# One instruction per step on both blocks of a unit's h, in a pair of PSUM banks, and the reciprocal held in SBUF

## The chip, the cores and the metric

The kernel runs on one core of one Trainium2 chip. The metric is the time of one execution in microseconds (us) on the device: the median of three runs of the kernel before is 825.93 us (825.08 to 829.08). Five engines work side by side, each through its own queue in order: TensorE (PE in the profile, with PEld for its loads of stationary data), VectorE (DVE), ScalarE (ACT), GpSimd (POOL) and SyncE (SP), which issues all of this kernel's DMAs. They meet only at semaphores. Data lie in SBUF, and results of TensorE in PSUM, which has eight banks of 512 fp32 values in each of 128 partitions.

## The reference

Two attentions and a layer with a rational function in place of an activation, all in fp32:

```python
def sm_attn(qq, kk, vv):
    s = scale * np.matmul(qq, kk.transpose(0, 1, 3, 2))
    a = np.exp(s - np.max(s, axis=-1, keepdims=True))
    return np.matmul(a / (np.sum(a, axis=-1, keepdims=True) + 1e-09), vv)
p_packed = sm_attn(p, k, v)               # 32 packed queries per head
x = sm_attn(q, p_packed, p_packed)        # 8 batches, 8 heads of 64, 576 rows each -> 4608 x 512
h = x @ w_in                              # 512 -> 2048
P = a[0] + a[1] * h + a[2] * h**2 + a[3] * h**3
Q = 1.0 + np.abs(b[0]) * np.abs(h) + np.abs(b[1]) * h**2
out = (P / (Q + 1e-6)) @ w_out            # 2048 -> 512
```

The weights come as 64-bit words and are taken apart into fp32 on the chip.

## The kernel before

**Units.** The work behind the attention is cut into 128 units: 8 batches, two halves of 288 rows each (HALF), and 8 chunks of 256 of the 2048 columns of h. `hidden` (line 644) builds one unit as a generator with yields in between. A unit has two blocks, f = 0 and 1, of 128 columns of h. For each block TensorE adds six matmuls (w_in and x are each split into a high and a low part, and three of the four products are taken) into one bank `h` of 128 x 288 values; there are two such banks (h_ring, line 299). From each block, one after the other, lines 659 to 664:

- ScalarE writes Y = a3*h + a2 and U = |b0*h|, and, after the first ten units, the square b1*h*h into a buffer `sq`;
- VectorE makes Y = Y*h and then Y = (Y + a1)*h.

So each of these instructions works on 288 columns and is issued twice in a unit. Behind both blocks, GpSimd adds U and sq (line 670), and from here all work on 576 columns at once: ScalarE writes V = ln(U + 1) and V = exp(-V) (lines 674, 675), a first reciprocal of Q, and VectorE takes three steps: Y = (Y + a0)*V, V = (U + 1)*V, and Y = (2 - V)*Y (lines 676, 677, 679), the numerator times the reciprocal with a step of refinement. **V lies in PSUM**, in the one pair of banks of V_ring (line 300). At last `split` (line 371) rounds Y to a high part gh on ScalarE and takes gl = Y - gh on GpSimd, and GpSimd copies the last 32 of the 288 rows' values to G, to be multiplied later (`remainder`). In the first ten units ("early": while the weights are still converted) no square is taken; there VectorE makes U = (U + b0)*h for each block (line 668) and ScalarE its absolute value, so GpSimd adds nothing.

`acc_block` (line 719) multiplies gh and gl by the parts of w_out, three units later (LAG), into two banks `acc`.

**Around it.** `attention` (line 456) of the next batch, and `m_chunk`, which multiplies the packed values by w_in, are put between the units and use the two banks `at`. `convert` (line 375) takes the words of the weights apart in the first 150 us: on VectorE with a shift-and-or (`w<-w`, `m<-m`) and an integer addition (`w<-w,w`, `win<-w,win`, `win<-m,win`) on 128 x 1024 words, each with two operands in SBUF.

**The order.** All operations go to a planner (lines 32 to 202), not straight to the engines. It knows a cost for each (line 40) and the dependences (line 100; in PSUM any two accesses of one buffer by different engines are ordered, in the order in which the code states them, reads too: line 120), plays a list schedule forward and backward four times, and issues in the order of the best. An instruction on one engine costs it the same whatever the other engines are doing. Buffers go round in rings (line 218): two for U, three for Y, one for sq and one pair of banks for V.

The eight banks are: two acc, two h, two V, two at.

Of the kernel before, what the change touches and what calls it, by code (L numbers as in the profile page):

```python
# [14 lines left out]
F32R = mybir.dt.float32r  # L15
# [3 lines left out]
AF = mybir.ActivationFunctionType  # L19
ALU = mybir.AluOpType  # L20
# [3 lines left out]
P = 128  # L24
# [209 lines left out]
def attention_rational_ffn(  # L234
# [32 lines left out]
    sb = ctx.enter_context(tc.tile_pool(name="sb", bufs=1))  # L267
    ps = ctx.enter_context(tc.tile_pool(name="ps", bufs=1, space=PSUM))
    tc.nc.scalar.preload_act_table_set("natural_log_exp_and_others")
    nc = Planner(tc.nc)  # L270


    ident = sb.tile([P, P], F32, name="ident")
    make_identity(tc.nc, ident)
    neg = sb.tile([P, P], F32R, name="neg")
    ab, abS, one, root = (sb.tile([P, n], F32, name=x) for n, x in ((6, "ab"), (7, "abS"), (1, "one"), (5, "root")))
    win = sb.tile([P, NCH, NCC, CF], F32, name="win")
    G = sb.tile([P, NFC, 2 * REM], F32, name="G")
# [4 lines left out]
    o_ring = Ring(sb, "o", 1, [P, 2, DM])  # L283

    full_ring = Ring(sb, "full", 1, [P, DM])
    nat_ring = Ring(sb, "nat", 2, [P, 4 * NS * D])
    pn_ring = Ring(sb, "pn", 1, [P, NG, D])
    rkq_ring = Ring(sb, "rkq", 1, [P, H, D])
    rv_ring = Ring(sb, "rv", 1, [REM, H, D])

    kx_ring = Ring(sb, "kx", 1, [P, NJ, T])
    ppT_ring = Ring(sb, "ppT", 2, [P, P])
    AH_ring, AL_ring = (Ring(sb, x, 2, [P, NG, T], F32R) for x in ("AH", "AL"))

    m_ring = Ring(sb, "m", NCH // 2, [P, 2, NG, 2 * CF], F32R)
    U_ring, U2_ring, Y_ring = (Ring(sb, x, n, [P, 2, HALF]) for x, n in (("U", 2), ("sq", 1), ("Y", 3)))
    gh_ring, gl_ring = (Ring(sb, x, 2, [P, 2, HMAIN], F32R) for x in ("gh", "gl"))
    acc_ring = Ring(ps, "acc", 2, [P, DM])
    h_ring = Ring(ps, "h", 2, [P, 512])
    V_ring = Ring(ps, "V", 1, [P, 2, 512])  # L300
    at_ring = Ring(ps, "at", 2, [P, 512])


# [107 lines left out]
    def load(bb, what):  # L411
        if bb >= B:
            return
        if what == "rem":

            r, rv, pn = NAT[bb, "r"], NAT[bb, "rv"], NAT[bb, "p"] = rkq_ring.next(), rv_ring.next(), pn_ring.next()
            nc.sync.dma_start(r[0:REM], k[bb, :, NS * P : T, :].rearrange("h p d -> p h d"))
            for j in range(NJ):
                nc.sync.dma_start(pn[32 * j : 32 * j + 32], p[bb, NG * j : NG * j + NG].rearrange("r n d -> n r d"))
            nc.sync.dma_start(r[REM : 2 * REM], q[bb, :, NS * P : T, :].rearrange("h p d -> p h d"))  # L420
            nc.sync.dma_start(rv, v[bb, :, NS * P : T, :].rearrange("h p d -> p h d"))
            return
# [32 lines left out]

    def attention(bb):
        pT, eTr, m2, st = (small[:, x:y] for x, y in zip(cuts, cuts[1:]))
        eTr = eTr[0:REM]
        m2 = m2.rearrange("p (a b) -> p a b", a=3)

        mx, nb, sm, f, fs, F = (st[:, 4 * i : 4 * i + 4] for i in range(6))
# [61 lines left out]
        for r in range(NG):  # L523
            t = bank(bb)
            for s in range(NS):
                nc.tensor.transpose(t[:, s * P : (s + 1) * P], KX[:, r, s * P : (s + 1) * P], ident)
            nc.scalar.copy(KX[:, 2 + r, 0 : NS * P], t)
            if r == 1:
                t = bank(bb)
                for i in range(NG):  # L530
                    nc.tensor.transpose(t[0:REM, i * P : (i + 1) * P], KX[:, i, NS * P : T], ident)
                nc.scalar.copy(eTr, t[0:REM, 0 : NG * P])
            yield

        t = bank(bb)
# [1 line left out]
        for r in range(NG):  # L537
            for x, blocks in enumerate((range(2), range(2, NS + 1))):
                o = slice((2 * r + x) * D, (2 * r + x + 1) * D)
                tiles(  # L540
                    (
                        (
                            t[32 * j : 32 * j + 32, o],
                            KX[:, 2 + r, s * P + 32 * j : s * P + 32 * j + 32] if s < NS else eTr[:, r * P + 32 * j : r * P + 32 * j + 32],
                            NAT[bb, f"v{j // 2}"][:, 2 * (j % 2) + r, s, :] if s < NS else rv[:, 2 * j + r, :],
                        ),
                        dict(start=s == blocks[0], stop=s == blocks[-1]),
                    )
                    for s in blocks
                    for j in range(NJ)  # L550
                )
# [92 lines left out]
    def hidden(bb, x, c):  # L644
        ah, al = AH[bb], AL[bb]
        mh, ml = (M[bb, c // 2][:, i, :, c % 2 * CF : (c % 2 + 1) * CF] for i in range(2))
        early = converted < len(words)
        U, V, Y = U_ring.next(), V_ring.next()[:, :, 0:HALF], Y_ring.next()
        U2 = None if early else U2_ring.next()
        for f in range(2):  # L650
            h = h_ring.next()[:, 0:HALF]
            for i, (w, a) in enumerate(((mh, ah), (ml, ah), (mh, al))):
                for g in range(NG):
                    nc.tensor.matmul(
                        h, w[:, g, f * P : (f + 1) * P], a[:, g, x * HALF : (x + 1) * HALF],
                        start=g == 0 and i == 0, stop=g == NG - 1 and i == 2,
                    )
            u, y = U[:, f, :], Y[:, f, :]
            nc.scalar.activation(y, h, AF.Identity, scale=reg_a3, bias=a2)
            nc.scalar.activation(u, h, AF.Abs, scale=reg_b1 if early else reg_b0)  # L660
            if not early:
                nc.scalar.activation(U2[:, f, :], h, AF.Square, scale=reg_root)
            nc.vector.tensor_mul(y, y, h)
            nc.vector.scalar_tensor_tensor(y, y, a1, h, ALU.add, ALU.mult)


            if early:
                nc.vector.scalar_tensor_tensor(u, u, b0, h, ALU.add, ALU.mult)
            elif f == 1:
                nc.gpsimd.tensor_add(U, U, U2)  # L670
            yield
        if early:
            nc.scalar.activation(U, U, AF.Abs)
        nc.scalar.activation(V, U, AF.Ln, bias=one)
        nc.scalar.activation(V, V, AF.Exp, scale=-1.0)
        nc.vector.scalar_tensor_tensor(Y, Y, a0, V, ALU.add, ALU.mult)
        nc.vector.scalar_tensor_tensor(V, U, (1.0 + 1e-6) * S, V, ALU.add, ALU.mult)
        yield
        nc.vector.scalar_tensor_tensor(Y, V, 2.0, Y, ALU.subtract, ALU.mult, reverse0=True)
        gh, gl = GS[bb, x, c] = gh_ring.next(), gl_ring.next()  # L680
        split(Y[:, :, 0:HMAIN], gh, gl)
# [91 lines left out]
    def stage(u):  # L773
        if u in pipe:
            next(pipe[u])

    def filler(i):
        if i in mt:
            m_chunk(*mt[i])
        for x in fill.get(i, ()):  # L780
            next(x)

    for u in range(NU + LAG + 2):
        if u < NU:
            pipe[u] = hidden(*units[u])
        stage(u)
        if 0 <= u - LAG < NU:
            acc_block(u - LAG, 0)
        filler(2 * u)
        stage(u)  # L790
        stage(u - 2)
# [39 lines left out]
```

## Time and profile before

| | |
|---|---|
| median of the runs, us | 825.93 |
| lowest and highest of the runs, us | 825.08, 829.08 |
| the profiled execution's own time, us | 828.38 |
| its span (first to last instruction), us | 826.6 |
| granted TensorE clock, mean | 0.965 |
| PE, PEld busy, us | 768.0, 605.5 |
| DVE, ACT, POOL busy, us | 694.3, 690.4, 459.5 |

A row of the profile that groups instructions names line, engine, operation, out<-in by the program's names, shapes out<-in, and the count; then the busy time of the group in us, the mean of one instruction in ns, and the idle time of the engine just before them with what ended it. All instructions have the line 202, since the planner issues them there; they are told apart by names. `Y<-Y,abS,V` is the step with a0 (abS holds the coefficients), `V<-U,V` and `Y<-V,Y` the two behind it, `Y<-Y,h` and `Y<-Y,abS,h` the two on h.

### The profile page before, as it was taken

To read this page: it belongs to the slowest core of one execution; us is meant where nothing else is said; L and a number is where in the kernel's file an instruction comes from. 1 tells how busy PE (TensorE), PEld (TensorE's weight loads), DVE (VectorE), ACT (ScalarE), POOL (GpSimd) and SP (SyncE) were. 2 spreads that over 40 slices of the span, in tenths; PEclk is the share of its full clock that TensorE was granted. 3 is DMA by queue.
4 is the path that set the end of the run, shared out by engine and by line. 5 is a ranking of instruction groups with operands and counts; after the bars stand their busy time and mean duration, and the time that the engine had idled before them with its cause. 6 is when DMAs were issued, how large, how long until landed. Compare 5 with 4: busy or idle time off the path is not lost.

```text
span 826.6 us, 15104 instructions
## 1 busy us (share of the span) xinstructions
PE 768.0 (93%) x5424; PEld 605.5 (73%) x5424; DVE 694.3 (84%) x1296; ACT 690.4 (84%) x1558; POOL 459.5 (56%) x454
## 2 busy tenths in 40 slices
PE   5467688899999999999999999999999999999997
PEld 3244365687877788788878788788877878778885
DVE  1899998888898688988898788988898778998873
ACT  3799787799988889899888888999888878898872
POOL 0003644675568445665577455765568446856663
PEclk9797698899999999999999999999999999999999
DMA  8994344001410116010510206010600211000001
GB/s 179 329 307 124 114 98 90 26 26 56 95 54 0 56 39 122 27 52 30 110 38 1 78 17 122 26 55 27 123 27 1 77 40 28 26 1 26 26 1 38
DMA packets 99834, 56.01 MB, mean 68 GB/s; under 512 B 82736, under 2 KB 90928, under 8 KB 99760
## 3 DMA queue, kind: packets, MB, share of 16 engines
q1 hardware_dynamic: 99760, 55.06, 25.2%
q8 instruction: 42, 0.69, 0.4%
q14 instruction: 32, 0.26, 0.1%
HBM read 45.62 MB, written 9.44 MB: 67 GB/s over the span
## 4 chain that ended last, share of the span: by engine, by line
PE 75%; DVE 12%; ACT 9%; issue 2%; DMA 1%; POOL 1%; SPq 0%; DVEq 0%; ACTq 0%; POOLq 0%
PE acc L202 37%; PE h L202 22%; PE at L202 16%; DVE Y L202 4%; DVE w L202 3%; DVE small L202 2%; ACT Y L202 1%; ACT U L202 1%; ACT V L202 1%; ACT m L202 1%; ACT w L202 1%; ACT kx L202 1%; DVE V L202 1%; DVE m L202 1%; ACT gh L202 1%
## 5 line engine op out<-in xcount | busy, mean ns | idle before, releaser
L202 PE MATMUL acc<-w,gh 128*128 128x512 f32 x1024 | 332.3, 403 | 9.6 <-ACT w L202 8.4
L202 PEld LDWEIGHTS acc<-w,gh 128*128 128x128 f32 x1024 | 187.0, 191 | 51.9 <-ACT w L202 10.4
L202 POOL TENSOR_TENSOR U<-U,sq 128x576 f32<-128x576 f32 x118 | 168.8, 1430 | 80.8 <-ACT sq L202 30.7
L202 PE MATMUL h<-AH,m 128*128 128x288 f32 x1024 | 195.9, 310 | 13.3 <-DVE Y L202 7.2
L202 POOL TENSOR_TENSOR gl<-Y,gh 128x512 fp32r<-128x512 f32 x128 | 169.7, 1326 | 67.3 <-ACT gh L202 28.0
L202 PEld LDWEIGHTS h<-AH,m 128*128 128x128 f32 x1024 | 161.5, 194 | 55.2 <-DVE Y L202 26.5
L202 PE MATMUL acc<-w,gl 128*128 128x512 f32 x512 | 196.1, 398 | 0.0
L202 ACT ACTIVATE Y<-h,abS 128x288 f32<-128x288 f32 x256 | 127.8, 513 | 19.3 <-PE h L202 17.1
L202 DVE TENSOR_TENSOR Y<-Y,h 128x288 f32<-128x288 f32 x256 | 111.0, 448 | 38.5 <-ACT sq L202 18.3
L202 DVE SCALAR_TENSOR_TENSOR Y<-Y,abS,V 128x576 f32<-128x576 f32 x128 | 103.4, 808 | 40.5 <-ACT V L202 39.9
L202 ACT ACTIVATE sq<-h 128x288 f32<-128x288 f32 x236 | 97.6, 421 | 40.4 <-PE h L202 35.2
L202 POOL COPY G<-Y 128x64 f32<-128x64 f32 x128 | 31.7, 247 | 177.7 <-DVE Y L202 155.7
L202 DVE SCALAR_TENSOR_TENSOR Y<-Y,abS,h 128x288 f32<-128x288 f32 x256 | 126.3, 508 | 3.2
L202 PEld LDWEIGHTS acc<-w,gl 128*128 128x128 f32 x512 | 96.8, 190 | 25.2 <-issue 6.9
L202 PE MATMUL h<-AL,m 128*128 128x288 f32 x512 | 114.3, 302 | 0.0
L202 ACT ACTIVATE U<-h 128x288 f32<-128x288 f32 x256 | 100.4, 425 | 5.2 <-DVE V L202 2.8
L202 ACT ACTIVATE V<-U,one 128x576 f32<-128x576 f32 x128 | 98.9, 773 | 3.0 <-DVE Y L202 2.4
L202 DVE SCALAR_TENSOR_TENSOR Y<-V,Y 128x576 f32<-128x576 f32 x128 | 96.0, 750 | 2.0
L202 DVE SCALAR_TENSOR_TENSOR V<-U,V 128x576 f32<-128x576 f32 x128 | 96.2, 752 | 0.0
L202 ACT CAST gh<-Y 128x512 fp32r<-128x512 f32 x128 | 81.9, 640 | 6.2 <-DVE Y L202 5.0
L202 PEld LDWEIGHTS h<-AL,m 128*128 128x128 f32 x512 | 85.5, 194 | 1.2 <-issue 0.4
L202 ACT ACTIVATE V<-V 128x576 f32<-128x576 f32 x128 | 85.9, 671 | 0.4
(122 smaller groups left out, 886.3 us busy)
## 6 DMA issues: line engine op xcount, KB each, us to landing
nat<-in_k_dram SPq DMA_DIRECT2D x16, 512.0 KB, 5.0
out_dram<-o SPq DMA_DIRECT2D x15, 512.0 KB, 2.7
w<-in_moe_w_out_dram SPq DMA_DIRECT2D x14, 512.0 KB, 5.2
nat<-in_v_dram SPq DMA_DIRECT2D x14, 512.0 KB, 4.0
nat<-in_q_dram SPq DMA_DIRECT2D x14, 512.0 KB, 6.1
m<-in_moe_w_in_dram SPq DMA_DIRECT2D x8, 512.0 KB, 10.1
w<-in_moe_w_in_dram SPq DMA_DIRECT2D x8, 512.0 KB, 7.4
rkq<-in_k_dram SPq DMA_DIRECT2D x8, 128.0 KB, 4.8
```

Source lines behind the costliest of these rows:

```text
L202: getattr(getattr(self.nc, engine), name)(*args, **kwargs)
```

## The change

Both blocks of h now lie in one pair of banks, 128 x 2 x 288 values, and there are two such pairs. The pair that V had in PSUM is given up; V lies in SBUF, in a ring of two buffers of its own, and the square is written into V first, so that sq is gone. Each of the steps on h is one instruction on 576 columns instead of two on 288, stated when both blocks are done. In the code, ScalarE's square now stands behind VectorE's first product with h, and before VectorE's second.

The room in SBUF comes from two places. The values v of the last 64 rows (`rv`) were 64 partitions with eight heads; they are now 128 partitions with four heads, loaded by two DMAs, and the transposed weights that go with them (`eTr`) are put into both halves of the partitions, by transposing the last 128 columns and then overwriting the lower 64 partitions: two more 128 x 128 transposes per batch. And `neg`, the negative identity that the early `m_chunk` needs, takes the buffer `full` before others use it. In the main loop the stage of two units ago is now stated before this unit's second.

```diff
-    neg = sb.tile([P, P], F32R, name="neg")
+    neg = full_ring.next([P, P], F32R)
-    rv_ring = Ring(sb, "rv", 1, [REM, H, D])
+    rv_ring = Ring(sb, "rv", 1, [P, H // 2, D])
-    U_ring, U2_ring, Y_ring = (Ring(sb, x, n, [P, 2, HALF]) for x, n in (("U", 2), ("sq", 1), ("Y", 3)))
+    U_ring, V_ring, Y_ring = (Ring(sb, x, n, [P, 2, HALF]) for x, n in (("U", 2), ("V", 2), ("Y", 3)))
-    h_ring = Ring(ps, "h", 2, [P, 512])
-    V_ring = Ring(ps, "V", 1, [P, 2, 512])
+    h_ring = Ring(ps, "h", 2, [P, 2, 512])
...
-            nc.sync.dma_start(rv, v[bb, :, NS * P : T, :].rearrange("h p d -> p h d"))
+            for i in range(2):
+                src = v[bb, 4 * i : 4 * i + 4, NS * P : T, :].rearrange("h p d -> p h d")
+                nc.sync.dma_start(rv[REM * i : REM * (i + 1)], src)
...
                 for i in range(NG):
-                    nc.tensor.transpose(t[0:REM, i * P : (i + 1) * P], KX[:, i, NS * P : T], ident)
-                nc.scalar.copy(eTr, t[0:REM, 0 : NG * P])
+                    o = slice(i * P, (i + 1) * P)
+                    nc.tensor.transpose(t[:, o], KX[:, i, T - P : T], ident)
+                    nc.tensor.transpose(t[0:REM, o], KX[:, i, NS * P : T], ident)
+                nc.scalar.copy(eTr, t[:, 0 : NG * P])
...
-        U, V, Y = U_ring.next(), V_ring.next()[:, :, 0:HALF], Y_ring.next()
-        U2 = None if early else U2_ring.next()
+        U, V, Y = U_ring.next(), V_ring.next(), Y_ring.next()
+        h = h_ring.next()[:, :, 0:HALF]
         for f in range(2):
-            h = h_ring.next()[:, 0:HALF]
...
-            u, y = U[:, f, :], Y[:, f, :]
-            nc.scalar.activation(y, h, AF.Identity, scale=reg_a3, bias=a2)
-            nc.scalar.activation(u, h, AF.Abs, scale=reg_b1 if early else reg_b0)
-            if not early:
-                nc.scalar.activation(U2[:, f, :], h, AF.Square, scale=reg_root)
-            nc.vector.tensor_mul(y, y, h)
-            nc.vector.scalar_tensor_tensor(y, y, a1, h, ALU.add, ALU.mult)
-            if early:
-                nc.vector.scalar_tensor_tensor(u, u, b0, h, ALU.add, ALU.mult)
-            elif f == 1:
-                nc.gpsimd.tensor_add(U, U, U2)
-            yield
+            if f == 0:
+                yield
+        nc.scalar.activation(Y, h, AF.Identity, scale=reg_a3, bias=a2)
+        nc.scalar.activation(U, h, AF.Abs, scale=reg_b1 if early else reg_b0)
+        nc.vector.tensor_mul(Y, Y, h)
+        if early:
+            nc.vector.scalar_tensor_tensor(U, U, b0, h, ALU.add, ALU.mult)
+        else:
+            nc.scalar.activation(V, h, AF.Square, scale=reg_root)
+        nc.vector.scalar_tensor_tensor(Y, Y, a1, h, ALU.add, ALU.mult)
+        yield
         if early:
             nc.scalar.activation(U, U, AF.Abs)
+        else:
+            nc.gpsimd.tensor_add(U, U, V)
```

Two places show what the planner makes of it. The first is VectorE in the middle of the run, at unit 65 of 128 (in a name like Y1_65 the number behind the letter is the buffer and the next one counts its uses; m2 and full belong to `m_chunk` and `remainder`). Before:

```order
L202 TENSOR_TENSOR Y1_65_891<-Y1_65_891,h0_129_893 128x288
L202 SCALAR_TENSOR_TENSOR Y1_65_891<-Y1_65_891,abS_69,h0_129_893 128x288
L202 TENSOR_TENSOR Y1_65_891<-Y1_65_891,h1_130_894 128x288
L202 SCALAR_TENSOR_TENSOR Y1_65_891<-Y1_65_891,abS_69,h1_130_894 128x288
L202 SCALAR_TENSOR_TENSOR Y0_64_881<-Y0_64_881,abS_69,V0_64_880 128x576
L202 TENSOR_TENSOR m2_23_897<-at1_154_898,m2_23_897 128x512
L202 SCALAR_TENSOR_TENSOR V0_64_880<-U1_64_879,V0_64_880 128x2x288
L202 TENSOR_TENSOR m2_23_897<-at0_155_899,m2_23_897 128x512
L202 SCALAR_TENSOR_TENSOR Y0_64_881<-V0_64_880,Y0_64_881 128x576
```

With the change, from the same unit's first product with h to its last step:

```order
L202 TENSOR_TENSOR Y1_65_773<-Y1_65_773,h0_65_774 128x576
L202 TENSOR_TENSOR m2_23_777<-at1_154_778,m2_23_777 128x512
L202 TENSOR_TENSOR m2_23_777<-at0_155_779,m2_23_777 128x512
L202 SCALAR_TENSOR_TENSOR Y1_65_773<-Y1_65_773,abS_68,h0_65_774 128x576
L202 TENSOR_TENSOR Y2_66_782<-Y2_66_782,h1_66_783 128x576
L202 SCALAR_TENSOR_TENSOR Y1_65_773<-Y1_65_773,abS_68,V0_65_772 128x576
L202 TENSOR_TENSOR full0_5_753<-at1_158_794,full0_5_753 128x512
L202 SCALAR_TENSOR_TENSOR V0_65_772<-U0_65_771,V0_65_772 128x576
L202 SCALAR_TENSOR_TENSOR Y2_66_782<-Y2_66_782,abS_68,h1_66_783 128x576
L202 SCALAR_TENSOR_TENSOR Y1_65_773<-V0_65_772,Y1_65_773 128x576
```

The four instructions on h of 288 columns are two of 576; V stays one instruction for each step, but its operand is now in SBUF like U and Y; and the next unit's product with h has moved in between this unit's own steps.

The second place is ScalarE at the same unit, from its first reading of h to the logarithm's neighbourhood. Before (sq is the square's buffer):

```order
L202 ACTIVATE sq0_55_892<-h0_129_893 128x288
L202 ACTIVATE Y1_65_891<-h0_129_893,abS_69 128x288
L202 ACTIVATE U0_65_889<-h0_129_893 128x288
L202 ACTIVATE V0_64_880<-U1_64_879,one_70 128x2x288
L202 ACTIVATE Y1_65_891<-h1_130_894,abS_69 128x288
L202 ACTIVATE U0_65_889<-h1_130_894 128x288
L202 ACTIVATE sq0_55_892<-h1_130_894 128x288
L202 CAST gh0_63_895<-Y2_63_870 128x512
L202 ACTIVATE V0_64_880<-V0_64_880 128x2x288
```

With the change (the square is the V that reads h; the V that reads U is the logarithm):

```order
L202 ACTIVATE Y1_65_773<-h0_65_774,abS_68 128x576
L202 ACTIVATE U0_65_771<-h0_65_774 128x576
L202 CAST m2_23_777<-at1_154_778 128x512
L202 CAST m2_23_777<-at0_155_779 128x512
L202 ACTIVATE V0_65_772<-h0_65_774 128x576
L202 CAST gh1_64_791<-Y0_64_765 128x512
L202 COPY kx0_6_784<-at1_156_788 128x512
L202 COPY kx0_6_784<-at0_157_789 128x512
L202 ACTIVATE V0_65_772<-U0_65_771,one_69 128x576
```

Six readings of h are three, and between the second and the third the planner has put two other casts, for the square now has to wait for VectorE's first product.

More of the change, by code (lines that the diff above doesn't have):

```diff
@@ L457, in attention @@
         pT, eTr, m2, st = (small[:, x:y] for x, y in zip(cuts, cuts[1:]))
-        eTr = eTr[0:REM]
         m2 = m2.rearrange("p (a b) -> p a b", a=3)
@@ L543, in attention @@
                             t[32 * j : 32 * j + 32, o],
-                            KX[:, 2 + r, s * P + 32 * j : s * P + 32 * j + 32] if s < NS else eTr[:, r * P + 32 * j : r * P + 32 * j + 32],
-                            NAT[bb, f"v{j // 2}"][:, 2 * (j % 2) + r, s, :] if s < NS else rv[:, 2 * j + r, :],
+                            KX[:, 2 + r, s * P + 32 * j : s * P + 32 * j + 32]
+                            if s < NS
+                            else eTr[REM * (j // 2) : REM * (j // 2 + 1), r * P + 32 * j : r * P + 32 * j + 32],
+                            NAT[bb, f"v{j // 2}"][:, 2 * (j % 2) + r, s, :]
+                            if s < NS
+                            else rv[REM * (j // 2) : REM * (j // 2 + 1), 2 * (j % 2) + r, :],
                         ),
@@ L654, in hidden @@
                     nc.tensor.matmul(
-                        h, w[:, g, f * P : (f + 1) * P], a[:, g, x * HALF : (x + 1) * HALF],
+                        h[:, f, :], w[:, g, f * P : (f + 1) * P], a[:, g, x * HALF : (x + 1) * HALF],
                         start=g == 0 and i == 0, stop=g == NG - 1 and i == 2,
                     )
-            u, y = U[:, f, :], Y[:, f, :]
-            nc.scalar.activation(y, h, AF.Identity, scale=reg_a3, bias=a2)
-            nc.scalar.activation(u, h, AF.Abs, scale=reg_b1 if early else reg_b0)
-            if not early:
-                nc.scalar.activation(U2[:, f, :], h, AF.Square, scale=reg_root)
-            nc.vector.tensor_mul(y, y, h)
-            nc.vector.scalar_tensor_tensor(y, y, a1, h, ALU.add, ALU.mult)
-            if early:
-                nc.vector.scalar_tensor_tensor(u, u, b0, h, ALU.add, ALU.mult)
-            elif f == 1:
-                nc.gpsimd.tensor_add(U, U, U2)
-            yield
+            if f == 0:
[9 more added lines that the diff above has]
+        yield
         if early:
             nc.scalar.activation(U, U, AF.Abs)
+        else:
+            nc.gpsimd.tensor_add(U, U, V)
         nc.scalar.activation(V, U, AF.Ln, bias=one)
@@ L789, in attention_rational_ffn @@
         filler(2 * u)
+        stage(u - 2)
         stage(u)
-        stage(u - 2)
         stage(u - 1)
```

## The prediction

> **What bounds the kernel now.** I first read the chain of waits, then the busy time by stretches, then the groups of instructions of the long middle part. The chain that ended last, by engine:
>
> ```profile
> PE 75%; DVE 12%; ACT 9%; issue 2%; DMA 1%; POOL 1%; SPq 0%; DVEq 0%; ACTq 0%; POOLq 0%
> ```
>
> Three stretches of the run, each with its length, then the busy time (and number of instructions) of PE, PEld, DVE, ACT, POOL, then the granted clock:
>
> ```profile
> 50.00:100.00 50.00, 31.00 (x196) 20.05 (x196) 50.00 (x69) 45.51 (x88) 21.16 (x16) 0.79 0.49 154
> 63.00:130.00 67.00, 48.65 (x356) 33.60 (x354) 65.04 (x95) 57.28 (x111) 34.23 (x25) 0.83 0.42 112
> 200.00:800.00 600.00, 597.49 (x4240) 480.82 (x4239) 513.74 (x982) 521.39 (x1213) 371.01 (x370) 1.00 0.18 46
> ```
>
> From 200 to 800 us TensorE is busy all the time (597.49 of 600) and DVE and ACT are not (86% and 87%); there PE is the bound. From 50 to 100 us DVE is busy in all 50.00 us: the conversion of the weights sits on it, and PE has 31.00. So the time is two stages: a start that VectorE sets, and a middle that TensorE sets. The instructions of the middle on DVE, and those on POOL:
>
> ```profile
> L202 DVE SCALAR_TENSOR_TENSOR Y<-Y,abS,h 128x288 f32<-128x288 f32 x213 | 105.2, 508 | 3.0
> L202 DVE TENSOR_TENSOR Y<-Y,h 128x288 f32<-128x288 f32 x213 | 92.3, 448 | 35.1 <-ACT sq L202 18.3 <-ACT U L202 10.7 <-ACT Y L202 2.6
> L202 DVE SCALAR_TENSOR_TENSOR Y<-Y,abS,V 128x576 f32<-128x576 f32 x106 | 85.6, 808 | 33.6 <-ACT V L202 33.0
> L202 DVE SCALAR_TENSOR_TENSOR V<-U,V 128x576 f32<-128x576 f32 x107 | 80.5, 752 | 0.0
> L202 DVE SCALAR_TENSOR_TENSOR Y<-V,Y 128x576 f32<-128x576 f32 x107 | 80.3, 751 | 1.8
> ```
>
> ```profile
> L202 POOL TENSOR_TENSOR U<-U,sq 128x576 f32<-128x576 f32 x106 | 151.7, 1431 | 74.7 <-ACT sq L202 30.5 <-ACT U L202 21.4 <-DVE Y L202 15.8
> L202 POOL TENSOR_TENSOR gl<-Y,gh 128x512 fp32r<-128x512 f32 x107 | 138.4, 1293 | 47.3 <-issue 22.6 <-ACT gh L202 13.8 <-POOL G L202 8.6
> L202 POOL COPY G<-Y 128x64 f32<-128x64 f32 x107 | 25.4, 237 | 93.9 <-DVE Y L202 74.6 <-DVE small L202 13.9 <-ACT kx L202 5.1
> ```
>
> 107 units pass in 600 us: 5.61 us for a unit. DVE is busy 513.74/107 = 4.80 us of it, POOL 371.01/107 = 3.47 us (62% of the time).
>
> **What the trace says of V's new place.** This decides the case. With V in PSUM, every DVE instruction of a unit has one operand in PSUM and one in SBUF. With V in SBUF, the last three have both in SBUF. Such instructions stand in the trace already: the conversion's shift-and-or and its integer addition, at the start. While POOL had nothing to do, they took this:
>
> ```profile
> L202 DVE SCALAR_TENSOR_TENSOR m<-m 128x1024 int32<-128x1024 int32 x4 | 4.9, 1214 | 0.0
> L202 DVE CUSTOM_DVE_ANT_0 win<-m,win 128x2048 uint16<-128x2048 uint16 x4 | 4.8, 1199 | 0.0
> ```
>
> From 63 to 130 us, where POOL works too, the same instructions are longer, and so are POOL's (first DVE's groups, then POOL's):
>
> ```profile
> L202 DVE SCALAR_TENSOR_TENSOR w<-w 128x1024 int32<-128x1024 int32 x9 | 13.7, 1524 | 0.0
> L202 DVE CUSTOM_DVE_ANT_0 w<-w,w 128x2048 uint16<-128x2048 uint16 x7 | 10.5, 1504 | 0.0
> L202 DVE CUSTOM_DVE_ANT_0 win<-w,win 128x2048 uint16<-128x2048 uint16 x2 | 3.9, 1972 | 0.0
> ```
>
> ```profile
> L202 POOL TENSOR_TENSOR w<-w,w 128x512 fp32r<-128x512 f32 x12 | 18.4, 1553 | 7.6 <-ACT w L202 5.6 <-issue 1.9
> L202 POOL TENSOR_TENSOR gl<-Y,gh 128x512 fp32r<-128x512 f32 x7 | 13.2, 1888 | 12.9 <-ACT gh L202 11.6 <-issue 1.2
> L202 POOL COPY G<-Y 128x64 f32<-128x64 f32 x6 | 2.7, 457 | 12.6 <-DVE Y L202 9.9 <-DVE small L202 2.7
> ```
>
> The timeline shows how (start, length):
>
> ```profile
> 63.45 1.29 POOL L202 TENSOR_TENSOR gl<-Y,gh 128x512 fp32r<-128x512 f32 x1 [2.86 <-ACT gh L202]
> 63.61 2.23 DVE L202 SCALAR_TENSOR_TENSOR w<-w 128x1024 int32<-128x1024 int32 x1
> ...
> 85.36 2.42 POOL L202 TENSOR_TENSOR gl<-Y,gh 128x512 fp32r<-128x512 f32 x1 [1.18 <-issue]
> 85.40 1.21 DVE L202 SCALAR_TENSOR_TENSOR w<-w 128x1024 int32<-128x1024 int32 x1
> 86.54 0.80 DVE L202 SCALAR_TENSOR_TENSOR Y<-Y,abS,V 128x576 f32<-128x576 f32 x1
> 87.27 1.60 DVE L202 SCALAR_TENSOR_TENSOR w<-w 128x1024 int32<-128x1024 int32 x1
> ```
>
> The first DVE instruction ends 1.10 us after gl's end at 64.74, about its own length: it waited for all of gl. The second time DVE is undisturbed, and gl, which takes 1.29 us alone, ends 1.17 us after DVE's end at 86.61. Then `Y<-Y,abS,V`, with V in PSUM, runs beside gl in its usual 0.80 us, and the shift-and-or at 87.27 waits again until gl is done at 87.78. So an instruction of DVE with two operands in SBUF and one of POOL exclude each other, and one operand in PSUM avoids it. None of the middle's rows shows this: gl has 1293 ns there.
>
> The Trainium skill says so as a rule ("SBUF — State Buffer", section "Who interferes with whom"): a DVE instruction with two SBUF inputs shares its second read port with GpSimd, and whichever issues second blocks until the first is done. It speaks against this change, and by it alone, with whole instructions, the port would be taken 3.47 + 2.31 = 5.78 us in each unit of 5.61, some 20 us more in 118 units. The trace agrees that they exclude each other (the rows above).
>
> **The change part by part.** The sum is made against the profiled execution's 828.4 us, which lies 2.4 above the median of the runs.
>
> *Waits for POOL.* In the 67 us above, 18 such DVE instructions took 13.7 + 10.5 + 3.9 = 28.1 us in place of 18 x 1.21 = 21.8: 0.35 us more for each. POOL was busy 51% of that stretch, of which some was its own waiting: 12 x 0.26 + 7 x 0.60 + 6 x 0.22 = 8.6 us by the rows' means against 1293 and 237, so 38% was work. In the middle POOL works 3.47 us per unit, 58% of a unit of 5.95 us (the result below). Scaled by the one share 0.35 becomes 0.40, by the other 0.53. I take 0.45 us, nearer to the first, whose share is the one that DVE met. Three instructions: 1.35 us per unit.
>
> *Fewer instructions on DVE.* Two of 448 and two of 508 ns go: 1.91 us. One each of 752 and 808 come (rows of 576 columns, without and with a coefficient): 1.56. Rows overlap by 0.07 us (85.40 + 1.21 against 86.54), which two fewer instructions lose: 0.35 - 0.14 = 0.21 us saved. So DVE has 4.80 - 0.21 + 1.35 = 5.94 us per unit, more than the 5.61 in which PE goes round. It has 1.02 us to spare without the waits, so the turning point is 0.34 us per instruction. With DVE busy all the time, as in 50 to 100 us, the middle and end lose 0.33 x 118 = 39 us. Were it busy 97% (65.04 of 67), the unit would be 6.12 and the loss 60.
>
> *The start.* The ten early units have, besides, this:
>
> ```profile
> L202 DVE SCALAR_TENSOR_TENSOR U<-U,abS,h 128x288 f32<-128x288 f32 x20 | 10.0, 501 | 0.0
> ```
>
> Two of 501 become one of 808, less the overlap: 0.12 us. They save 10 x (0.21 + 0.12) = 3 us and wait 30 x 0.35 = 10.5: 7 us lost on the engine that sets this stage.
>
> *ScalarE.* The rows of the middle:
>
> ```profile
> L202 ACT ACTIVATE Y<-h,abS 128x288 f32<-128x288 f32 x213 | 105.8, 510 | 14.1 <-PE h L202 13.0 <-issue 0.2
> L202 ACT ACTIVATE sq<-h 128x288 f32<-128x288 f32 x212 | 87.5, 420 | 33.3 <-PE h L202 28.6 <-POOL gl L202 4.1
> L202 ACT ACTIVATE U<-h 128x288 f32<-128x288 f32 x214 | 83.6, 422 | 5.0 <-DVE V L202 2.6 <-PE h L202 2.0
> L202 ACT ACTIVATE V<-U,one 128x576 f32<-128x576 f32 x107 | 82.5, 771 | 1.2 <-DVE Y L202 0.8
> L202 ACT ACTIVATE V<-V 128x576 f32<-128x576 f32 x106 | 70.9, 669 | 0.3
> ```
>
> ```profile
> L202 ACT ACTIVATE U<-U 128x576 f32<-128x576 f32 x10 | 7.1, 710 | 0.0
> ```
>
> Six readings of h, 2 x (510 + 422 + 420) = 2.70 us, become one of about 771 (with a bias) and two of 669: 2.11. The logarithm and the exponential now stay in SBUF, as the early U<-U does (710 against 669): 0.08 given back. It saves 0.51 us per unit, and nothing of the time: ACT was not the bound. The new wait, of the square for DVE's first product, holds up the casts and logarithms queued behind it; ACT's 0.7 us per unit of idle time (600 - 521.39, by 107) and the 0.51 cover it. If they didn't, 0.45 us, one of DVE's waits, would come to 53 us in 118 units.
>
> *TensorE.* Two more transposes per batch, 16 in all, of which a row is:
>
> ```profile
> L202 PE MATMUL at<-ident,kx 128*128 128x128 f32 x48 | 7.3, 273 | 0.0
> ```
>
> 7.3/48 = 0.15 us each, 2.4 us in all: hidden once DVE is the bound, 2.4 us lost if PE remains it. In return the waits for a bank of h shrink, of which the longest is below with the wait for V:
>
> ```profile
> PEld h L202 <- DVE Y L202: 26.5, 44, 2.2
> DVE Y L202 <- ACT V L202: 39.9, 57, 1.6
> ```
>
> With two pairs, PE can fill one while the other is read. Up to 26.5 us would be gained, but only while PE is the bound; I count none.
>
> *The rest.* The second DMA for rv is one more issue per batch on SP's queue, ahead of loads of the next batch and of outputs; the values are needed tens of us later, and nothing on the chain is SP's (SPq 0%): nothing, and at worst the row's landing time, 5.9 us, in the first batch alone:
>
> ```profile
> rv<-in_v_dram SPq DMA_DIRECT2D x8, 128.0 KB, 5.9
> ```
>
> The stage's new place and neg's new room only shift the order; nothing. At the end the last unit's first block no longer runs ahead of its second: 0.26 + 0.25 + 0.25 on ACT and 0.3 on DVE, about 1 us.
>
> Sum: 39 + 7 + 1 = 47; 828.4 + 47 - 2.4 = **873 us**.
>
> **The rivals.** *The waits fit into DVE's idle time.* If POOL and DVE happen to fall beside each other, and an instruction waits under 0.34 us, PE stays the bound: 0.35 unscaled is just there, and gives 829, less whatever of the waits for h PE gets back: 818 to 832, about 826. For it: the planner's order alternates steps on h with those on V. Against: POOL works a larger share of the time in the middle than in the 67 us.
>
> *The waits do not come at all*, because fp32 operands do not collide as the conversion's integers do; no fp32 instruction of two SBUF operands lies beside POOL's work in this trace. Then DVE falls to 4.59 us per unit, PE stays the bound, half of the 26.5 us comes back, and the start gains 3: 826 - 13 - 3 + 2 = 812. It would be faster. Against: POOL's own gl is fp32 and waited for the integers.
>
> *The chain of a unit becomes the bound.* V is now held from the square on: 0.67 (square) + 1.43 (POOL) + 0.77 + 0.67 (ln, exp) + 2.31 (DVE) = 5.9 us, plus 1.35 of waits and every queue on the way, with two buffers: at 12 us held, 6.0 us per unit, it decides. At 13.4 the unit takes 6.7: + 1.09 x 118 = 129, about 960. For it: four engines in turn, with a wait now in two of them. Against: 5 us of queues would be needed.
>
> **How the numbers follow.** The forecast gets 0.66, the fit into idle time 0.14, no waits 0.10, the chain 0.10. Half a per cent, 4 us, is about what a measurement of this kernel can tell from no change. Of the second case I put 0.05 below that, 0.06 within and 0.03 above. Faster: 0.10 + 0.05 = 0.15; same 0.06; slower 0.66 + 0.10 + 0.03 = 0.79. The forecast's own ends are 829 (0.35 us per wait) and, with 0.53 and DVE 97% busy, 6.18/0.97 = 6.37 us per unit: 828.4 + 90 + 8 - 2.4 = 924. The range takes 820, for most of the second case, to 912, leaving out the other two and the forecast's last tenth.
>
> **What would show it.** In the middle the groups Y<-Y,abS,V, V<-U,V and Y<-V,Y together would rise from 2.31 to about 3.7 us per unit, gl and U on POOL above their 1293 and 1431 ns, DVE's busy share to over 95% and PE's below it, with the chain passing to DVE and POOL. If those rows keep their lengths, the argument is wrong; if they rise and PE stays at 99%, the waits were hidden.

## The result and the profile after

The changed kernel takes 912.8 us (911.96 to 914.94) against 827.5 us of the kernel before on the same chip: 1.104 times as long, with a 95% interval of 1.100 to 1.108. The direction was forecast, the size not: 85 us were lost, 47 forecast, and the time lies 0.8 us above the range's end of 912.

The profiled execution has a span of 910.2 us, 83.6 more than before. Its middle, in the same columns as before (length; busy time of PE, PEld, DVE, ACT, POOL; clock):

```profile
200.00:800.00 600.00, 561.62 (x3929) 433.67 (x3930) 532.26 (x705) 452.30 (x811) 386.14 (x329) 0.99 0.18 45
```

TensorE has fallen from 597.49 to 561.62 us and is no longer busy all the time. But VectorE has not taken its place: it is busy 532.26 us, 89%, less than TensorE's 94%. The groups from 200 to 880 us, first DVE's, then POOL's:

```profile
L202 DVE SCALAR_TENSOR_TENSOR V<-U,V 128x576 f32<-128x576 f32 x108 | 128.9, 1194 | 4.9
L202 DVE SCALAR_TENSOR_TENSOR Y<-Y,abS,V 128x576 f32<-128x576 f32 x108 | 117.6, 1089 | 20.0 <-ACT V L202 19.5
L202 DVE SCALAR_TENSOR_TENSOR Y<-V,Y 128x576 f32<-128x576 f32 x108 | 114.0, 1055 | 1.7
L202 DVE SCALAR_TENSOR_TENSOR Y<-Y,abS,h 128x576 f32<-128x576 f32 x108 | 86.8, 804 | 24.6 <-ACT V L202 24.3
L202 DVE TENSOR_TENSOR Y<-Y,h 128x576 f32<-128x576 f32 x107 | 79.4, 742 | 23.1 <-ACT U L202 12.7 <-issue 5.1 <-ACT Y L202 2.8
```

```profile
L202 POOL TENSOR_TENSOR U<-U,V 128x576 f32<-128x576 f32 x108 | 177.0, 1638 | 42.2 <-ACT V L202 39.2 <-ACT small L202 2.2
L202 POOL TENSOR_TENSOR gl<-Y,gh 128x512 fp32r<-128x512 f32 x108 | 149.6, 1385 | 46.3 <-POOL G L202 33.8 <-ACT gh L202 7.5 <-issue 4.7
L202 POOL COPY G<-Y 128x64 f32<-128x64 f32 x107 | 35.4, 331 | 142.7 <-DVE Y L202 121.4 <-ACT V L202 10.8 <-DVE small L202 5.8
```

108 units in 680 us are 6.30 us for a unit, 0.69 more than before; at that pace 118 units lose 81 us. The three steps on V, of 752, 808 and 751 ns before, now take 1194, 1089 and 1055: 1.03 us of waits in a unit, 0.34 for each. POOL's three are longer too, by 0.21, 0.09 and 0.09 us. The two steps on h, with an operand in PSUM, have just the length of 576 columns. So in a unit VectorE is busy 5.59 us (532.26 over the 95.2 units that fit into 600 us) and idle 0.71.

The timeline shows the meetings (start, length):

```profile
403.07 1.29 POOL L202 TENSOR_TENSOR gl<-Y,gh 128x512 fp32r<-128x512 f32 x1 [0.49 <-POOL G L202]
403.56 1.42 DVE L202 SCALAR_TENSOR_TENSOR Y<-Y,abS,V 128x576 f32<-128x576 f32 x1 [0.54 <-ACT V L202]
...
404.32 1.93 POOL L202 TENSOR_TENSOR U<-U,V 128x576 f32<-128x576 f32 x1
...
404.90 0.80 DVE L202 SCALAR_TENSOR_TENSOR Y<-Y,abS,h 128x576 f32<-128x576 f32 x1
```

VectorE's step starts while gl runs, gl is done at 404.36, and the step ends 0.62 us later, at 404.98, though it takes 0.81 us alone and had started 0.80 us before gl's end. GpSimd's addition has started at 404.32 and ends 1.27 us after the step, though it takes 1.43 alone. So each has waited for the other's end, but for the first 0.15 to 0.2 us of its own length. The step on h at 404.90 runs beside the addition in its usual 0.80 us.

The longest waits of one engine for another now have these among them (total, times, longest):

```profile
ACT U L202 <- DVE V L202: 61.5, 50, 2.5
DVE Y L202 <- ACT V L202: 51.8, 58, 3.1
ACT gh L202 <- DVE Y L202: 46.1, 49, 3.2
```

ScalarE waits for VectorE to have read U for the last time, and VectorE for the exponential; so each of these two has idle time that the other causes. Before, the second wait was 39.9 us.

### The profile page after: what moved, and what is told of

It reads as the page before. It is cut to its first block, busy times and chain, and to the rows that moved or that the text cites. A ratio compares the mean times of both kernels' runs of the same rounds, so it can differ in the third digit from the quotient of the medians.

```text
span 910.2 us, 14669 instructions
## 1 busy us (share of the span) xinstructions
PE 800.1 (88%) x5440; PEld 608.8 (67%) x5440; DVE 787.7 (87%) x1030; ACT 670.8 (74%) x1184; POOL 528.3 (58%) x454
## 5 line engine op out<-in xcount | busy, mean ns | idle before, releaser
L202 POOL TENSOR_TENSOR U<-U,V 128x576 f32<-128x576 f32 x118 | 194.2, 1645 | 44.1 <-ACT V L202 41.0
L202 POOL COPY G<-Y 128x64 f32<-128x64 f32 x128 | 46.0, 360 | 238.2 <-DVE Y L202 214.4
L202 DVE SCALAR_TENSOR_TENSOR Y<-Y,abS,V 128x576 f32<-128x576 f32 x128 | 141.0, 1102 | 27.3 <-ACT V L202 26.9
L202 DVE SCALAR_TENSOR_TENSOR V<-U,V 128x576 f32<-128x576 f32 x128 | 152.0, 1188 | 5.2
L202 DVE SCALAR_TENSOR_TENSOR Y<-V,Y 128x576 f32<-128x576 f32 x128 | 132.9, 1038 | 1.9
L202 ACT ACTIVATE U<-h 128x576 f32<-128x576 f32 x128 | 83.3, 651 | 66.0 <-DVE V L202 61.5
L202 DVE SCALAR_TENSOR_TENSOR Y<-Y,abS,h 128x576 f32<-128x576 f32 x128 | 102.9, 804 | 25.4 <-ACT V L202 25.0
L202 DVE TENSOR_TENSOR Y<-Y,h 128x576 f32<-128x576 f32 x128 | 95.1, 743 | 25.7 <-ACT U L202 14.6
L202 ACT ACTIVATE Y<-h,abS 128x576 f32<-128x576 f32 x128 | 94.9, 742 | 14.5 <-PE h L202 10.2
L202 ACT ACTIVATE V<-h 128x576 f32<-128x576 f32 x118 | 76.6, 649 | 20.7 <-DVE Y L202 20.0
```

What stands on the lines that cost most here:

```text
L202: getattr(getattr(self.nc, engine), name)(*args, **kwargs)
```

## Experiments: what the loss comes from

The theory: VectorE's three steps and GpSimd's instructions that read SBUF exclude each other. The rivals: the merged steps on h make a unit's chain longer, and the waits only fill idle time; or the rest of the change has a part.

**e1_split: V in SBUF, merging undone.**

```diff
-    h_ring = Ring(ps, "h", 2, [P, 2, 512])
+    h_ring = Ring(ps, "h", 4, [P, 512])
...
+        for f in range(2):
+            h, u, v2, y = hs[f], U[:, f, :], V[:, f, :], Y[:, f, :]
...
+            if not early:
+                nc.scalar.activation(v2, h, AF.Square, scale=reg_root)
+            nc.vector.tensor_mul(y, y, h)
```

> The merging is undone and V stays in SBUF: four single banks for h, each step on h issued for 288 columns again, the square into V as in the change. Theory (V in SBUF meets GpSimd): the three steps on V stay at 1.0 to 1.2 us each, and the time stays at 890 to 925 us. Rival (the coarser steps on h and their order make a unit's chain longer, the meetings only fill time that was idle): 826 to 850 us.

Measured: 941.9 us, 1.139 times before (1.133 to 1.145). Between 200 and 800 us:

```profile
L202 DVE SCALAR_TENSOR_TENSOR V<-U,V 128x576 f32<-128x576 f32 x89 | 108.5, 1219 | 3.7
L202 DVE SCALAR_TENSOR_TENSOR Y<-V,Y 128x576 f32<-128x576 f32 x90 | 108.2, 1202 | 0.2
L202 DVE SCALAR_TENSOR_TENSOR Y<-Y,abS,V 128x576 f32<-128x576 f32 x89 | 93.4, 1049 | 39.9 <-ACT V L202 37.6
```

The rival falls: without the merging it is slower still, above the theory's own range, 116 us above the kernel before. What the merging is worth can't be read from e1 against the change, since e1 also states the square ahead of VectorE's products, as the kernel before does. The run e3 below has that order with merged steps and takes 932.5 us: against it the merging is worth 9 us (against the change's own 912.8 it would seem to be 29).

**e2_pool_writes and e5_fills_x3: GpSimd only writes.**

```diff
-            nc.gpsimd.tensor_add(U, U, V)
+            nc.gpsimd.memset(V, 0.0)
+            nc.gpsimd.memset(V, 1.0)
...
-        split(Y[:, :, 0:HMAIN], gh, gl)
+        nc.scalar.copy(gh, Y[:, :, 0:HMAIN])
+        nc.gpsimd.memset(gl.bitcast(F32), 0.0)
+        nc.gpsimd.memset(gl.bitcast(F32), 0.0)
```

> The changed kernel, but GpSimd reads nothing in the unit's chain: its addition of the square and its subtraction for gl are left out, and two fills (of V, and of gl) stand in the place of each, which only write. VectorE's three steps still have both operands in SBUF, and the steps on h are still merged. Theory (the two engines exclude each other): the three steps fall back to 0.75 to 0.81 us, apart from meetings with what GpSimd still reads, and the time to 815 to 850 us. Rival (merging): the steps may fall, the time stays above 870 us.

> As e2_pool_writes, but three fills stand in the place of each of GpSimd's two instructions, not two: 3 x 0.58 = 1.74 us for the addition and 3 x 0.53 = 1.58 us for the subtraction, longer than these take in the change with their waits (1.64 and 1.39 us). It asks whether e2 was fast because nothing met, or because GpSimd's part of a unit's chain was shorter. Theory (meetings): 822 to 845 us, VectorE's three steps at 0.83 to 0.92 us. Rival (the length of the chain through GpSimd): 870 to 915 us.

In both, the planner counts the fills that stand for one instruction at that instruction's cost.

Measured: e2 828.1 us, 1.0025 times before (1.0005 to 1.0045); e5, with three fills for each, 837.4, 1.013 (1.010 to 1.016). In e2 the three steps took 903, 836 and 839 ns, not the 0.75 to 0.81 us expected. The middle of e5, and its groups between 200 and 800 us, DVE's and POOL's:

```profile
200.00:800.00 600.00, 586.78 (x4159) 472.93 (x4159) 487.04 (x753) 485.74 (x872) 429.69 (x774) 1.00 0.18 46
```

```profile
L204 DVE SCALAR_TENSOR_TENSOR Y<-Y,abS,V 128x576 f32<-128x576 f32 x104 | 88.7, 853 | 32.6 <-ACT V L204 32.4
L204 DVE SCALAR_TENSOR_TENSOR Y<-V,Y 128x576 f32<-128x576 f32 x104 | 86.8, 835 | 1.5
L204 DVE SCALAR_TENSOR_TENSOR V<-U,V 128x576 f32<-128x576 f32 x104 | 82.4, 792 | 1.1
```

```profile
L204 POOL MEMSET V<- 128x576 f32 x312 | 181.1, 580 | 72.2 <-ACT V L204 60.0
L204 POOL MEMSET gl<- 128x512 f32 x310 | 163.1, 527 | 61.2 <-PE acc L204 50.4
```

The fills take 1.74 + 1.58 = 3.3 us in a unit, longer than the two instructions in the change with their waits (1.64 + 1.39 = 3.0), GpSimd is busy 429.69 us in place of 386.14, and yet 75 of the 85 us are gone. So it is GpSimd's reading that costs, not its busy time. For the chain of a unit this holds in its first part, where the fills of V wait for the square and the logarithm for the fills; the fills of gl wait for neither Y nor gh, so how long the chain is behind Y was not held fixed. The steps still wait 0.17 us in a unit; GpSimd's copies to G and its part of the attention still read, and I take these for the cause, which no run shows.

That steps and fills run at the same time can be seen at 401 us of e5 (start, length):

```profile
401.32 0.81 DVE L204 SCALAR_TENSOR_TENSOR Y<-Y,abS,V 128x576 f32<-128x576 f32 x1
...
401.63 1.86 POOL L204 MEMSET V<- 128x576 f32 x3 [0.80 <-ACT V L204]
...
402.77 0.75 DVE L204 SCALAR_TENSOR_TENSOR V<-U,V 128x576 f32<-128x576 f32 x1
```

Both steps have their operands in SBUF and keep their lengths beside the fills.

**e4_v_over_h: V in PSUM again, steps merged.**

```diff
-        U, V, Y = U_ring.next(), V_ring.next(), Y_ring.next()
-        h = h_ring.next()[:, :, 0:HALF]
+        U, V2, Y = U_ring.next(), V_ring.next(), Y_ring.next()
+        V = h = h_ring.next()[:, :, 0:HALF]
...
+        stage(u - 2)
         stage(u)
...
-        stage(u - 2)
         stage(u)
```

The last lines state the stage of two units ago ahead of both of this unit's stages; so e4 has an order of its own besides V's place.

> The changed kernel with V written over h, in h's own pair of PSUM banks, when h has been read; the square goes to the buffer in SBUF that was V's. The steps on V have one operand in PSUM again, the steps on h stay merged. A pair of banks is now held from the first matmul to V's last reading. Theory: the three steps fall back to 0.75 to 0.81 us; the hold of about 11 to 13 us with two pairs gives 5.6 to 6.5 us per unit, so 830 to 930 us, with TensorE's waits for h as the longest. Rival (merging): the steps fall and nothing else does, and the time stays at 905 to 920 us with the same waits as in the change.

Measured: 878.8 us, 1.063 (1.059 to 1.068). DVE's groups of the three steps on V (the first now holds both the step with a1 and the one with a0) and two of POOL's, between 200 and 800 us:

```profile
L202 DVE SCALAR_TENSOR_TENSOR Y<-Y,abS,h 128x576 f32<-128x576 f32 x197 | 155.8, 808 | 68.7 <-ACT V L202 63.1 <-ACT h L202 5.0
L202 DVE SCALAR_TENSOR_TENSOR Y<-h,Y 128x576 f32<-128x576 f32 x98 | 73.4, 749 | 1.7
L202 DVE SCALAR_TENSOR_TENSOR h<-U,h 128x576 f32<-128x576 f32 x98 | 73.6, 751 | 0.0
```

```profile
L202 POOL TENSOR_TENSOR U<-U,V 128x576 f32<-128x576 f32 x99 | 141.7, 1431 | 60.3 <-ACT V L202 60.1
L202 POOL TENSOR_TENSOR gl<-Y,gh 128x512 fp32r<-128x512 f32 x99 | 128.0, 1293 | 76.5 <-issue 41.5 <-POOL G L202 25.6 <-ACT gh L202 8.9
```

With V in PSUM no wait is left within these instructions on either engine. So V's place decides over the waits, in a kernel whose steps on h are merged. The time is another matter: the kernel is still slow without any of these waits, as the long hold of a pair let expect; that the hold sets it, and not the order, is argued, not shown.

**e12_rest_only: the rest of the change alone** (the diff of rv, eTr, neg and the stages' order, on the kernel before).

> The kernel before with only the rest of the change: rv in 128 partitions by two DMAs, the additional transposes, neg in the buffer of full, and the stages' order. h, V, sq and the steps on them are as before. Theory: 824 to 832 us, nothing that can be measured. Rival (this rest has a part in the loss): over 835 us.

Measured: 826.2 us, 0.999 (0.997 to 1.0005). The rest costs nothing.

**e3_square_first: the order of h's readers.**

```diff
         nc.scalar.activation(U, h, AF.Abs, scale=reg_b1 if early else reg_b0)
+        if not early:
+            nc.scalar.activation(V, h, AF.Square, scale=reg_root)
         nc.vector.tensor_mul(Y, Y, h)
```

> The changed kernel with the square stated ahead of VectorE's first product with h, so that ScalarE's three readings of h follow one another and no longer wait for VectorE in between. Theory (meetings): 900 to 922 us, within 1% of the change. Rival (the merged steps' order makes the chain longer; ScalarE waited 20 us for VectorE ahead of the square): 870 to 895 us.

Measured: 932.5 us, 1.129 (1.125 to 1.133): 20 us worse than the change, which neither expected. Taking ScalarE's wait for VectorE's first product away gains nothing. And the order of the same instructions alone moves 20 us.

## Experiments: why more was lost than the waits

The waits are 1.03 us in a unit, less than the 1.35 forecast, and VectorE had 1.02 us to spare. What leaves it idle 0.71 us?

**e6, e7, e8: more buffers**, on a ground without G, which makes room for them.

In e6:

```diff
-        nc.gpsimd.tensor_copy(G[:, 2 * c : 2 * c + 2, r0 : r0 + HREM], Y[:, :, HMAIN:HALF])
...
-        for x in rem.get(u, ()):
-            remainder(*x)
```

and on top of it in e8 (in e7 the 3 for U alone):

```diff
-    U_ring, V_ring, Y_ring = (Ring(sb, x, n, [P, 2, HALF]) for x, n in (("U", 2), ("V", 2), ("Y", 3)))
+    U_ring, V_ring, Y_ring = (Ring(sb, x, n, [P, 2, HALF]) for x, n in (("U", 3), ("V", 3), ("Y", 4)))
```

> The changed kernel without the last 32 rows of each half: the copy to G and the product behind it are left out, on all engines. It is the ground for e7 and e8, which need the room of G. GpSimd has some 0.5 us less per unit, TensorE 0.4 us, ScalarE and VectorE 0.1 us each. Theory (meetings lengthen a unit's chain, which closes over two buffers of U): fewer meetings, 870 to 900 us. Rival (VectorE with its waits is full): 885 to 905 us.

> As e6_no_g, with three buffers for U in place of two: one size is changed. In the change ScalarE waited 61.5 us for VectorE's last reading of U before it could write U again. Theory (the chain closes over two buffers of U): 20 to 60 us less than e6, and that wait is nearly gone. Rival (VectorE with its waits is full): within 1% of e6, other waits in its place.

> As e6_no_g, with three buffers for U, three for V and four for Y. Theory (buffers close the chain): 25 to 70 us less than e6, VectorE busy 93% or more between 200 and 800 us. Rival (VectorE with its waits is full): within 1% of e6.

Measured: 883.5, 878.9 and 871.2 us; 1.068 (1.065 to 1.072), 1.063 (1.060 to 1.066) and 1.053 (1.050 to 1.056). The wait for U, in e6

```profile
ACT U L202 <- DVE V L202: 73.6, 61, 2.9
ACT gh L202 <- DVE Y L202: 31.0, 39, 2.9
```

is not among e7's longest, where the second has taken its place:

```profile
ACT gh L202 <- DVE Y L202: 86.4, 74, 3.2
```

So the theory that the chain closes over U's buffers falls: a third one gives 5 us, all of them 12, and the waits move on. VectorE is busy 542.72 of 600 us in e8, 90%, not the 93% of that theory.

**e11_planned_waits: the planner is told.** No instruction changes, only what the planner believes.

```diff
+        if engine == "vector" and name == "scalar_tensor_tensor" and self.columns(aps[0]) == 2 * 288:
+            fixed += 340 * all(x.space != PSUM for x in aps)
+        if engine == "gpsimd" and self.columns(aps[0]) >= 512:
+            fixed += 150
```

> The changed kernel, with the measured waits in the planner's costs: 340 ns more for each of the three steps with both operands in SBUF, 150 ns more for GpSimd's long instructions. Only the order can change. Theory (meetings): 895 to 922 us. Rival (the planner's order, made without the waits, is what costs): below 890 us.

Measured: 884.8 us, 1.070 (1.067 to 1.072): 28 us less than the change, the rival's way. The middle:

```profile
200.00:800.00 600.00, 573.67 (x4041) 444.31 (x4040) 566.56 (x727) 469.05 (x838) 411.49 (x341) 1.00 0.19 46
```

VectorE is busy 94% instead of 89%. Its three steps, and the two waits of the change that were shown above:

```profile
L206 DVE SCALAR_TENSOR_TENSOR V<-U,V 128x576 f32<-128x576 f32 x98 | 111.4, 1136 | 1.2 <-DVE Y L206 0.5
L206 DVE SCALAR_TENSOR_TENSOR Y<-V,Y 128x576 f32<-128x576 f32 x98 | 110.0, 1123 | 0.9
L206 DVE SCALAR_TENSOR_TENSOR Y<-Y,abS,V 128x576 f32<-128x576 f32 x98 | 107.5, 1097 | 9.2 <-ACT V L206 8.9
```

```profile
ACT U L206 <- DVE V L206: 31.3, 25, 2.6
DVE Y L206 <- ACT V L206: 22.0, 39, 1.3
```

The steps wait as long as in the change, 1.05 us in a unit against 1.03. What the new order gives back is idle time: of the two waits between ScalarE and VectorE a half or less is left.

**e15 and e16: the told planner on the ground of e6 and of e8.**

> As e6_no_g, with the waits in the planner's costs as in e11. In e11 VectorE was busy 94% of the middle, in the change 89%. Theory (once the order knows the waits, VectorE with its waits is the bound, at 5.5 us of work and waits per unit here): 845 to 870 us, VectorE busy 94% or more. Rival (something else leaves VectorE idle): 872 to 884 us, busy share as in e6 (90%).

> As e15_no_g_planned, with three buffers for U and V and four for Y. Theory: 835 to 862 us, VectorE busy 96% or more, and the waits of the three steps at 0.25 to 0.4 us. Rival: 865 to 872 us, as e8 had it with the first costs.

Measured: 837.1 us, 1.014 (1.010 to 1.017), and 842.6 us, 1.017 (1.011 to 1.023). e15's middle, then e16's:

```profile
200.00:800.00 600.00, 573.50 (x4055) 440.80 (x4044) 579.55 (x750) 488.82 (x863) 402.04 (x246) 1.00 0.18 44
```

```profile
200.00:800.00 600.00, 569.24 (x4055) 447.25 (x4054) 593.81 (x747) 482.04 (x863) 381.28 (x244) 0.99 0.18 44
```

VectorE is busy 97% and 99%, as the prediction had assumed for the change, at 5.7 and 5.8 us for a unit. From e6 to e15, 46 us come from the order alone, and from e8 to e16 29. Since e3 moved 20 us by another order alone, one such gain could be chance; with e11 there are three, of 28, 46 and 29 us, and all go the same way. More buffers on top make VectorE busier and the kernel no faster; its intervals with e15 overlap. Both leave out G's work and still take 1.4 and 1.7% longer than the kernel before.

**e9 and e10, e13 and e14: one more reading on GpSimd, against a fill as long.**

In e9 one copy more in each unit, in e10 a fill in its place:

```diff
+        nc.gpsimd.tensor_copy(spare[:, 0, 0:384], spare[:, 1, 0:384])
```

```diff
+        nc.gpsimd.memset(spare[:, 0, :], 0.0)
```

In e13 and e14 the two go into V, and so have to wait for its last reading:

```diff
         split(Y[:, :, 0:HMAIN], gh, gl)
+        nc.gpsimd.tensor_copy(V[:, :, 0:192], spare[:, 0, 0:384].rearrange("p (a b) -> p a b", a=2))
```

```diff
         split(Y[:, :, 0:HMAIN], gh, gl)
+        nc.gpsimd.memset(V, 0.0)
```

> As e6_no_g, and in each unit GpSimd copies 384 columns from one spare buffer to another, which nothing needs and which waits for nothing: some 0.55 us that read SBUF. Theory (what GpSimd and the three steps take in turn sets the pace, wherever in the chain it stands): 0.4 to 0.6 us more per unit, 925 to 960 us. Rival (the chain of a unit sets the pace, and GpSimd has a third of its time idle): 883 to 900 us.

> As e9_extra_read, with a fill of the spare buffer (576 columns, 0.58 us) in the place of the copy: as long, but it reads nothing. Theory (meetings): 880 to 900 us, well under e9. Rival (any instruction more in GpSimd's queue delays the chain): as e9.

> As e6_no_g, with a copy on GpSimd of 384 columns of a spare buffer into V, behind V's last reading in each unit, so that it stands in the middle of the run too and not at the start alone, as e9's copies did. Nothing needs it; it reads SBUF, some 0.55 us. Theory (meetings, in the middle): VectorE's three steps wait 0.1 to 0.2 us more in a unit each and GpSimd's instructions too, 0.15 to 0.4 us more per unit: 900 to 930 us. Rival (only the length of GpSimd's queue or of V's hold counts): as e14.

> As e13_chain_read, with a fill of V (576 columns, 0.58 us) in the place of the copy: at the same place, as long, reading nothing. Theory (meetings): 880 to 897 us, at least 12 us under e13. Rival (queue and hold): within 6 us of e13.

Measured: 901.0 us in e9 against 884.3 in e10 (1.089, 1.086 to 1.093; 1.069, 1.067 to 1.072). But nothing held the copies and fills back, and the planner put all 128 before 200 us. The busy time in e9 of the instructions that touch the spare buffer (DVE, then POOL, with their number):

```profile
50.00:100.00 50.00, 0.00 (x0) 36.07 (x42) 0.69 0.39 131
...
200.00:800.00 600.00, 0.00 (x0) 0.00 (x0) 0.98 0.18 45
```

The pair speaks of the start alone: there, against e6, the copies cost 17 us and the fills 1. At the place in the middle, e13 and e14 give 890.2 and 889.6 us, 1.079 (1.074 to 1.085) and 1.076 (1.070 to 1.080): no difference, against the theory. The rows of the copy in e13 and of the fill in e14 between 200 and 800 us:

```profile
L206 POOL COPY V<-spare 128x384 f32<-128x384 f32 x96 | 50.7, 528 | 137.3 <-DVE Y L206 110.5 <-DVE small L206 26.8
```

```profile
L206 POOL MEMSET V<- 128x576 f32 x96 | 55.7, 580 | 144.2 <-DVE Y L206 117.4 <-DVE small L206 26.7
```

The copy stands behind the unit's last step on V, when VectorE often turns to a product with h; that it therefore meets little is argued, not shown. How much a reading costs depends on where it falls.

## Why the prediction was right in direction and wrong in size

- **The two engines exclude each other, in fp32 as in the conversion's integers, and V in PSUM avoids it: right.** The rows of the change, e2 and e5 (reading), and e4 (V's place) show it. The Trainium skill's rule ("SBUF — State Buffer", "Who interferes with whom") holds here, also where it exempts GpSimd instructions that only write: e5's fills kept 580 and 527 ns beside steps of 0.79 to 0.85 us.
- **The price of a step's waits: 0.45 us forecast, 0.34 measured.** The rows of the start, 0.35 unscaled, were nearer than the scaling by POOL's share. The work without waits was right: 4.59 us forecast, 5.59 - 1.03 = 4.56 measured.
- **The step that failed: "With DVE busy all the time, as in 50 to 100 us, the middle and end lose 0.33 x 118 = 39 us."** The sum gave 5.94 us of work and waits; measured are 5.59 busy and 0.71 idle, 6.30, so 81 us. The sum put the idle time at nothing, and that was the mistake: VectorE, busy 5.59 us in a unit, has no more to do than the 5.61 us in which TensorE went round before, and is still not the bound. The 50.00 of 50 us were taken from the conversion, whose rows have 0.0 us of idle time ahead of them; the steps of a unit waited for ScalarE already in the kernel before (33.6 us ahead of `Y<-Y,abS,V`). And the order had been planned without the waits. In each engine's queue something stands behind an instruction that is later than planned, and the delay is handed on (ScalarE for VectorE, VectorE for ScalarE, above). With the waits in the plan, VectorE fills up to 94%, and without G's work to 97%, and 28 and 46 us come back, while the waits within the steps stay. In e11 it is still idle for 600 - 566.56 = 33 us of the middle; what leaves it so is open. More buffers closed such a gap without G's work (e16), but the kernel was no faster for it; with G's work they were not tried, for want of room.
- **That the direction came out owes something to luck.** With the measured price the same sum gives 4.59 + 1.03 = 5.62 us, 0.01 above TensorE's 5.61, and so no loss in the middle worth naming. The forecast's 39 us stood on a price that was too high; the loss that came has another source, the idle time.
- **The start: 7 us forecast, none seen.** The eleventh unit's last step, behind which no conversion is left in either kernel, starts 0.6 us earlier than before. This step and the last unit's, before and then with the change:

```profile
156.93 0.74 DVE L202 SCALAR_TENSOR_TENSOR Y<-V,Y 128x576 f32<-128x576 f32 x1
...
813.38 0.76 DVE L202 SCALAR_TENSOR_TENSOR Y<-V,Y 128x576 f32<-128x576 f32 x1
```

```profile
156.30 0.74 DVE L202 SCALAR_TENSOR_TENSOR Y<-V,Y 128x576 f32<-128x576 f32 x1
...
897.42 0.76 DVE L202 SCALAR_TENSOR_TENSOR Y<-V,Y 128x576 f32<-128x576 f32 x1
```

The 117 units between take 741.12 us in place of 656.45, so 84.7 us more: the whole loss lies there.

- **ScalarE's work, TensorE's waits for h, the second DMA, the transposes: right to count nothing.** ScalarE is busy 452.30 of 600 us, and TensorE is no longer busy all the time; e12 covers the rest. Taking ScalarE's new wait for VectorE's first product away gained nothing (e3); but its wait for U belongs to the idle time above.
- **The rivals.** The waits were not hidden, though 0.34 us is just the turning point that was worked out: at the turning point an engine would have to be busy without a gap. The waits did come, against the second rival. The chain over two buffers, priced at 960, showed as ScalarE's wait of 61.5 us for U, but without G's work a third buffer for U gave 5 us (e7): it wasn't what set the pace there.
- **The signs.** The three steps rose from 2.31 to 3.34 us (3.7 forecast) and GpSimd's instructions too. But VectorE's share was to rise over 95% with TensorE's below it; it is 89%, and TensorE's 94%. This sign spoke against VectorE as the bound.

## What to carry to other kernels

Before an operand of a VectorE instruction moves from PSUM to SBUF, look at GpSimd's busy share, and price the meetings from places in the same trace where two-operand instructions already run beside it. Here a wait inside an instruction showed as busy time and as a longer mean (1055 ns for 751), so compare the means with rows that had no neighbour. Then add what the queues make of it: where an order is fixed beforehand, put the measured waits into its costs before judging the change; here that was worth a third of the loss.

## What the runs showed of the hardware that was not expected

A fill on GpSimd (580 ns for 576 columns) runs beside VectorE's steps with two operands in SBUF, and keeps its length; the step took 0.75 us beside it in e5. One instruction on 576 columns of two PSUM banks took 742 ns on VectorE and 650 on ScalarE, where two of 288 took 2 x 448 and 2 x 422.
